# p.v of a decode attention kernel: four keys a matmul, in four column tiles of the array

## The chip, the cores and the metric

The kernel runs on one core of one Trainium2 chip. The metric is device time in microseconds (us), the median of several executions. A profiled execution gives a trace; its span is about 1.7 us shorter than the device time of the same execution (842.7 us against 844.37 us for the kernel before).

Engines are named as the profile does: PE is TensorE's matmul, PEld its weight load, DVE is VectorE, ACT is ScalarE, POOL is GpSimd, SP is SyncE (which issues the loads).

## The reference

Two independent decode steps of attention, A and B, each for one new token and 32 heads of 128. A attends to all 16384 cached keys, B to the last 4096. The outputs (512 columns each) stand side by side.

```
q = (x @ wq) split into 32 heads
scores = q . k_cache * 128**-0.5        # A: 16384 keys a head, B: 4096
p = softmax(scores)
o = p @ v_cache                         # one row of 128 per head
out = o (32*128) @ wo                   # 512 columns
```

Nearly all the bytes are K and V: with wq and wo 352 MB of bf16, each byte read once.

## The kernel before

Keys lie on partitions: 128 partitions, 128 keys on each for a head of A, 32 for a head of B. Work goes in *units* (one head of A, or four of B; 4 MB of K and 4 MB of V each) and in *chunks* of 64 keys a partition, two a unit. K and V have two 4 MB buffers each. Per chunk: DVE multiplies K by q (prod) and adds the upper to the lower half (half), PE sums on with an identity matrix (red), DVE finishes the sum (sc), ACT takes exp and its sum (p, cs), PE multiplies p by V.

```python
def _red(nc, cx, ch):                      # 8 matmuls of 512 columns a chunk
    ...
        cx.o(nc.tensor.matmul(ch.red[:, :, :], lhsT=cx.ident[:, :],
                              rhs=ch.half[:, :, b * W : (b + 1) * W], ...))

def _pv(nc, cx, ch, i):
    k0, n, st, h, first, last = ch.pieces[i]
    ...
    for c in range(n):                     # one key of each partition a matmul
        cx.o(nc.tensor.matmul(
            o_ps[0:1, 0:DH],
            lhsT=ch.p[:, k0 + c : k0 + c + 1],
            rhs=ch.unit.vt[:, ch.k0 + k0 + c, :],
            start=(first and c == 0), stop=(last and c == n - 1), ...))
        if c == 0:
            ...                            # the sum of p (fp32, 1x1)
    if ch.last_of_unit and i == len(ch.pieces) - 1:
        cx.loads.release("vt")             # the next V load may be issued
```

At a head's end: reciprocal of the sum (DVE), a scaled copy to a row (ACT), four small matmuls that turn the row into a column (PE), a cast (DVE) for each four heads, and the product with wo (PE).

The softmax here doesn't subtract the row's maximum and nothing guards it: scores larger than these inputs give would overflow.

## Time and profile before

844.42 us, median of 3 (844.36 to 844.65). What matters, and where it is read:

| reading | value | view |
|---|---|---|
| load queue q1 | 352.33 MB, 98.2% of 16 DMA engines' span | DMA queues |
| instruction queue q8 | 49 packets, 0.80 MB, 0.4% | DMA queues |
| PE, DVE, ACT busy | 68%, 70%, 8% | busy time |
| p.v matmuls | 5120 of 128 columns, 335.4 us | groups |
| granted PE clock | 0.842 | run's result |

These are lines of the page of the kernel before: busy time in us (share, count of instructions), the DMA queues (packets, MB, share of 16 engines), the chain that ended last, and groups of instructions (count | busy us, mean ns of one | idle us of the engine just before them, and what ended most of it).

```profile
PE 576.0 (68%) x6336; PEld 410.8 (49%) x6336; DVE 587.3 (70%) x344; ACT 64.7 (8%) x275; POOL 0.8 (0%) x8
...
q1 hardware_dynamic: 21188, 352.33, 98.2%
q8 instruction: 49, 0.80, 0.4%
q14 instruction: 8, 0.07, 0.0%
...
DMA 65%; DVE 20%; issue 7%; PE 6%; SPq 0%; ACT 0%; DVEq 0%
...
L146 DVE TENSOR_TENSOR prod<-kt,qallA 128x8192 bf16<-128x8192 bf16 x64 | 283.0, 4422 | 207.4 <-DMA kt<-in_A_k_cache_dram 207.3
L203 PE MATMUL o_ps<-vt,p_sb 128*1 128x128 bf16 x5120 | 335.4, 230 | 56.4 <-DMA vt<-in_A_v_cache_dram 56.4
L203 PEld LDWEIGHTS <-p_sb 128*1 128x1 bf16 x5120 | 317.4, 89 | 44.2 <-issue 44.2
L171 PE MATMUL red<-half,ident 128*128 128x512 bf16 x640 | 203.9, 476 | 16.0 <-DVE half L158 15.9
```

The kernel is bound by its loads: the load queue fills the 16 DMA engines for 98.2% of the span, and the chain is mostly DMA.

The table by windows (columns: window, length, busy of PE, PEld, DVE, ACT, POOL with counts, granted clock, DMA share, GB/s) shows the end of the kernel before:

```profile
805.00:810.00 5.00, 5.00 (x71) 4.19 (x71) 4.96 (x4) 0.35 (x2) 0.00 (x0) 0.92 1.02 424
810.00:815.00 5.00, 4.85 (x72) 3.89 (x69) 5.00 (x4) 0.35 (x2) 0.00 (x0) 1.00 0.88 369
815.00:820.00 5.00, 3.77 (x44) 2.62 (x45) 5.00 (x4) 0.36 (x1) 0.00 (x0) 1.00 0.90 359
820.00:825.00 5.00, 3.99 (x49) 2.75 (x45) 3.05 (x3) 0.53 (x4) 0.00 (x0) 1.00 1.00 419
825.00:830.00 5.00, 5.00 (x94) 5.00 (x94) 0.85 (x2) 0.89 (x5) 0.00 (x0) 1.00 0.67 272
```

At 810 to 820 us the rate dips, as a V load waits for its buffer.

### The profile page before, as it was taken

Reading aid. Unit: us, or ns where it says so; the run is one execution under the profiler, and the core shown is the slowest. Engines: PE = TensorE matmul, PEld = TensorE weight load, DVE = VectorE, ACT = ScalarE, POOL = GpSimd, SP = SyncE. Lnnn points to the kernel's source line nnn. Section 1 sums busy time; section 2 is a strip of 40 time slices with the busy share of each in tenths; the row PEclk is TensorE's granted clock in tenths of the full one; section 3 lists DMA queues with packets and bytes.
Section 4 is the critical chain, followed back from the end, with each engine's and each line's share of the span. In section 5 each row is a group of like instructions: output and inputs, shape, how many; then the busy total and the mean of one; then the engine's idle time right before and its main releaser. Section 6 shows DMA issues by size and latency. Waiting matters only on the chain.

```text
span 842.7 us, 13703 instructions
## 1 busy us (share of the span) xinstructions
PE 576.0 (68%) x6336; PEld 410.8 (49%) x6336; DVE 587.3 (70%) x344; ACT 64.7 (8%) x275; POOL 0.8 (0%) x8
## 2 busy tenths in 40 slices
PE   3377756767577665777677764677676668577687
PEld 1144544545555445445555444445454445444466
DVE  0992937779477783777867685766957779377791
ACT  2001100000000000100000000000000000000001
POOL 0000000000000000000000000000000000000000
PEclk9699787898788897888878897888898887788889
DMA  9999999999999999999999999999999999999993
GB/s 384 437 422 429 430 420 434 429 436 424 416 437 430 428 428 417 436 426 422 438 426 424 435 412 437 430 425 437 425 415 433 433 427 431 415 432 433 428 390 155
DMA packets 21533, 353.20 MB, mean 419 GB/s; under 512 B 2530, under 2 KB 2532, under 8 KB 4836
## 3 DMA queue, kind: packets, MB, share of 16 engines
q1 hardware_dynamic: 21188, 352.33, 98.2%
q8 instruction: 49, 0.80, 0.4%
q14 instruction: 8, 0.07, 0.0%
q10 hardware_dynamic: 288, 0.00, 0.0%
HBM read 352.32 MB, written 0.00 MB: 418 GB/s over the span
## 4 chain that ended last, share of the span: by engine, by line
DMA 65%; DVE 20%; issue 7%; PE 6%; SPq 0%; ACT 0%; DVEq 0%
DMA kt<-in_A_k_cache_dram 52%; DVE prod L146 13%; DMA vt<-in_A_v_cache_dram 7%; DMA kt<-in_B_k_cache_dram 6%; DVE half L158 6%; PE o_ps L203 4%; PE red L171 1%; DVE sc L183 1%; DVE recip L227 0%; PE outB L258 0%; PE oc_ps L241 0%; SPq L136 0%; PE outA L258 0%; ACT orow L229 0%; ACT rowB L269 0%
## 5 line engine op out<-in xcount | busy, mean ns | idle before, releaser
L146 DVE TENSOR_TENSOR prod<-kt,qallA 128x8192 bf16<-128x8192 bf16 x64 | 283.0, 4422 | 207.4 <-DMA kt<-in_A_k_cache_dram 207.3
L203 PE MATMUL o_ps<-vt,p_sb 128*1 128x128 bf16 x5120 | 335.4, 230 | 56.4 <-DMA vt<-in_A_v_cache_dram 56.4
L203 PEld LDWEIGHTS <-p_sb 128*1 128x1 bf16 x5120 | 317.4, 89 | 44.2 <-issue 44.2
L171 PE MATMUL red<-half,ident 128*128 128x512 bf16 x640 | 203.9, 476 | 16.0 <-DVE half L158 15.9
L158 DVE TENSOR_TENSOR half<-prod 128x4096 bf16<-128x4096 bf16 x80 | 182.5, 2281 | 0.0
L241 PE MATMUL oc_ps<-one,orow 1*32 1x1 bf16 x256 | 16.1, 171 | 173.1 <-ACT orow L229 173.1
L171 PEld LDWEIGHTS <-ident 128*128 128x128 bf16 x640 | 67.0, 115 | 110.7 <-issue 68.1
L241 PEld LDWEIGHTS <-orow 1*32 1x32 bf16 x256 | 11.5, 111 | 184.8 <-ACT orow L229 183.6
L146 DVE TENSOR_TENSOR prod<-kt,qallB 128x4096 bf16<-128x4096 bf16 x32 | 72.2, 2289 | 1.5 <-DMA kt<-in_B_k_cache_dram 0.9
L187 ACT ACTIVATE p_sb<-sc 128x64 bf16<-128x64 f32 (+1 forms) x96 | 23.5, 244 | 637.7 <-DVE sc L183 637.7
L183 DVE TENSOR_REDUCE sc<-red 128x64 f32<-128x512 f32 x80 | 54.8, 685 | 4.4 <-PE red L171 4.4
L212 PEld LDWEIGHTS o_ps<-ones_col,cs 128*1 128x1 f32 x192 | 14.7, 89 | 56.3 <-issue 56.3
L229 ACT ACTIVATE orow<-o_ps,recip 1x128 bf16<-1x128 f32 x64 | 22.1, 356 | 100.7 <-DVE recip L227 100.7
L227 DVE RECIPROCAL recip<-o_ps 1x1 f32<-1x1 f32 x64 | 9.0, 148 | 18.3 <-PE o_ps L203 18.3
L212 PE MATMUL o_ps<-ones_col,cs 128*1 128x1 f32 x192 | 19.5, 171 | 0.0
L101 PE MATMUL q_ps<-wq_t,xbA 128*128 128x512 bf16 x32 | 9.1, 455 | 13.1 <-DMA wq_t<-in_A_wq_dram 13.1
L187 ACT ACTIVATION_READ_ACCUMULATOR p_sb<-sc 128x1 f32 x96 | 17.9, 186 | 0.0
L101 PEld LDWEIGHTS <-xbA 128*128 128x128 bf16 x32 | 3.6, 114 | 18.1 <-DVE xbA L81 8.5
L101 PE MATMUL q_ps<-wq_t,xbB 128*128 128x512 bf16 x32 | 8.2, 377 | 5.3 <-ACT qallB L108 4.7
L258 PE MATMUL outB<-wo_t,oc 128*1 128x512 bf16 x32 | 8.2, 379 | 0.3 <-DVE oc L252 0.3
L258 PE MATMUL outA<-wo_t,oc 128*1 128x512 bf16 x32 | 8.2, 379 | 0.0
L101 PEld LDWEIGHTS <-xbB 128*128 128x128 bf16 x32 | 3.1, 96 | 10.1 <-issue 7.2
(17 smaller groups left out, 21.5 us busy)
## 6 DMA issues: line engine op xcount, KB each, us to landing
kt<-in_A_k_cache_dram SPq DMA_DIRECT2D x32, 4096.0 KB, 28.0
vt<-in_A_v_cache_dram SPq DMA_DIRECT2D x31, 4096.0 KB, 28.0
kt<-in_B_k_cache_dram SPq DMA_DIRECT2D x32, 1024.0 KB, 24.2
vt<-in_B_v_cache_dram SPq DMA_DIRECT2D x31, 1024.0 KB, 25.6
wq_t<-in_A_wq_dram SPq DMA_DIRECT2D x1, 4096.0 KB, 12.3
wq_t<-in_B_wq_dram SPq DMA_DIRECT2D x1, 4096.0 KB, 24.1
wo_t<-in_A_wo_dram SPq DMA_DIRECT2D x4, 1024.0 KB, 29.2
wo_t<-in_B_wo_dram SPq DMA_DIRECT2D x4, 1024.0 KB, 30.4
```

What stands on the lines that cost most here:

```text
L101: cx.o(nc.tensor.matmul(q_ps[:, :], lhsT=st.xb[:, c, :], rhs=st.wq_t[:, c, j * 512 : (j + 1) * 512], start=(c == 0), stop=(c == KC - 1),))
L146: cx.o(nc.vector.tensor_tensor(out=ch.prod[:, k0 : k0 + n, :], in0=ch.unit.kt[:, ch.k0 + k0 : ch.k0 + k0 + n, :], in1=q.rearrange("p (o d) ...
L158: cx.o(nc.vector.tensor_tensor(out=ch.half[:, :, :], in0=ch.prod[:, :, 0 : DH // 2], in1=ch.prod[:, :, DH // 2 : DH], op=ALU.add,))
L171: cx.o(nc.tensor.matmul(ch.red[:, :, :], lhsT=cx.ident[:, :], rhs=ch.half[:, :, b * W : (b + 1) * W], start=(b == 0), stop=(b == nb - 1),))
L183: cx.o(nc.vector.tensor_reduce(out=sc[:, :], in_=ch.red[:, :, :], axis=AX.X, op=ALU.add))
L187: cx.o(nc.scalar.activation(out=ch.p[:, k0 : k0 + n], in_=sc[:, k0 : k0 + n], func=ACT.Exp, scale=SCALE, accum_out=ch.cs[:, i : i + 1],))
L203: cx.o(nc.tensor.matmul(o_ps[0:1, 0:DH], lhsT=ch.p[:, k0 + c : k0 + c + 1], rhs=ch.unit.vt[:, ch.k0 + k0 + c, :], start=(first and c == 0) ...
L212: cx.o(nc.tensor.matmul(o_ps[0:1, DH : DH + 1], lhsT=ch.cs[:, i : i + 1], rhs=cx.ones_col[:, 0:1], start=False, stop=last, skip_group_chec ...
L227: cx.o(nc.vector.reciprocal(recip[:, :], o_ps[0:1, DH : DH + 1]))
L229: cx.o(nc.scalar.activation(out=orow[:, :], in_=o_ps[0:1, 0:DH], func=ACT.Copy, scale=recip[0:1, 0:1]))
L241: cx.o(nc.tensor.matmul(st.oc_ps[32 * hp : 32 * hp + 32, j : j + 1], lhsT=orow_j[:, j, :], rhs=cx.one[0:1, 0:1], start=True, stop=True,))
L258: cx.o(nc.tensor.matmul(st.out_ps[0:1, :], lhsT=st.oc[:, j : j + 1], rhs=st.wo_t[i][:, g, j * st.DN : (j + 1) * st.DN], start=(h == G - 1 ...
```

## The change

Its intent is to take load off PE: 16 matmuls of 512 columns a chunk instead of 64 of 128. A matmul takes the p of four keys as weights (4 columns) and the V of the same four keys (512 columns). Of its 4x512 result only the four diagonal blocks of 1x128 are wanted; the rest is waste that costs no extra time here. Four such matmuls go to four column tiles of the array (output partitions 0, 32, 64, 96). At a head's end the bank is copied to SBUF and four fp32 matmuls with a selecting weight column pick and sum the diagonal blocks.

```diff
 def _pv(nc, cx, ch, i):
...
-    for c in range(n):
+    T = n // 4
+    for t in range(T):
+        r = 32 * (t % 4)
+        k = k0 + 4 * t
         cx.o(nc.tensor.matmul(
-            o_ps[0:1, 0:DH],
-            lhsT=ch.p[:, k0 + c : k0 + c + 1],
-            rhs=ch.unit.vt[:, ch.k0 + k0 + c, :],
...
+            acc[r : r + 4, :],
+            lhsT=ch.p[:, k : k + 4],
+            rhs=ch.unit.vt[:, ch.k0 + k : ch.k0 + k + 4, :],
+            start=(first and t < 4),
+            stop=(last and t >= T - 4),
         ))
...
+    if last:
+        st.acc_sb[h] = cx.accs_pool.tile([P, 4 * DH], F32, tag="accs", name="acc_sb")
+        cx.o(nc.scalar.copy(st.acc_sb[h][:, :], acc[:, :]))
+
+def _fin_fold(nc, cx, st, heads):
...                                        # the sums of p, as before, then
+        for e in range(4):
+            cx.o(nc.tensor.matmul(
+                f_ps[0:1, x, 0:DH],
+                lhsT=cx.sel[:, e : e + 1],
+                rhs=acc_sb[:, e * DH : (e + 1) * DH],
+                start=False, stop=(e == 3), skip_group_check=True,
+            ))
```

The rest of the diff sets up `sel` and the two zeroed PSUM banks `acc`, and reorders the steps at a head's end so that two heads of B share them.

More of the change, by code (lines that the diff above doesn't have):

```diff
@@ L199, in _pv @@
     if first:
-        st.o_ps[h] = cx.pso_pool.tile([1, DH + 1], F32, tag="o", name="o_ps")
-    o_ps = st.o_ps[h]
-    for c in range(n):
-        cx.o(nc.tensor.matmul(
-            o_ps[0:1, 0:DH],
-            lhsT=ch.p[:, k0 + c : k0 + c + 1],
-            rhs=ch.unit.vt[:, ch.k0 + k0 + c, :],
-            start=(first and c == 0),
-            stop=(last and c == n - 1),
-            skip_group_check=True,
-        ))
-        if c == 0:
-            cx.o(nc.tensor.matmul(
-                o_ps[0:1, DH : DH + 1],
-                lhsT=ch.cs[:, i : i + 1],
-                rhs=cx.ones_col[:, 0:1],
-                start=False,
-                stop=last,
-                skip_group_check=True,
-            ))
+        cx.turn = 1 - cx.turn
@@ L220, in _pv @@
+        st.acc[h], st.cs[h] = cx.acc[cx.turn], []
+    acc = st.acc[h]
+    st.cs[h].append(ch.cs[:, i : i + 1])
+    T = n // 4
+    for t in range(T):
+        r = 32 * (t % 4)
+        k = k0 + 4 * t
+        cx.o(nc.tensor.matmul(
+            acc[r : r + 4, :],
[3 more added lines that the diff above has]
+            stop=(last and t >= T - 4),
+        ))
     if ch.last_of_unit and i == len(ch.pieces) - 1:
@@ L221, in _pv @@
         cx.loads.release("vt")
-def _fin_row(nc, cx, st, h):
-    o_ps = st.o_ps.pop(h)
-    recip = cx.small.tile([1, 1], F32, tag="recip", name="recip")
-    cx.o(nc.vector.reciprocal(recip[:, :], o_ps[0:1, DH : DH + 1]))
-    orow = cx.small.tile([1, DH], BF16, tag="orow", name="orow")
-    cx.o(nc.scalar.activation(
-        out=orow[:, :], in_=o_ps[0:1, 0:DH], func=ACT.Copy, scale=recip[0:1, 0:1]
-    ))
-    st.orow[h] = orow
+    if last:
+        st.acc_sb[h] = cx.accs_pool.tile([P, 4 * DH], F32, tag="accs", name="acc_sb")
+        cx.o(nc.scalar.copy(st.acc_sb[h][:, :], acc[:, :]))
@@ new lines, in _fin_fold @@
+def _fin_fold(nc, cx, st, heads):
+    f_ps = cx.psf_pool.tile([1, 2, DH + 1], F32, tag="f", name="f_ps")
+    for x, h in enumerate(heads):
+        cs = st.cs.pop(h)
+        for i, col in enumerate(cs):
+            cx.o(nc.tensor.matmul(
+                f_ps[0:1, x, DH : DH + 1], lhsT=col, rhs=cx.ones_col[:, 0:1],
+                start=(x == 0 and i == 0), stop=(i == len(cs) - 1), skip_group_check=True,
+            ))
+        acc_sb = st.acc_sb.pop(h)
+        for e in range(4):
+            cx.o(nc.tensor.matmul(
+                f_ps[0:1, x, 0:DH],
+                lhsT=cx.sel[:, e : e + 1],
+                rhs=acc_sb[:, e * DH : (e + 1) * DH],
+                start=False, stop=(e == 3), skip_group_check=True,
+            ))
+    return f_ps
@@ L235, in _fin_col, with _fin_row @@
+def _fin_row(nc, cx, st, heads, f_ps):
+    n = len(heads)
+    recip = cx.small.tile([1, 2], F32, tag="recip", name="recip")
+    cx.o(nc.vector.reciprocal(recip[0:1, 0:n], f_ps[0:1, 0:n, DH]))
+    for x, h in enumerate(heads):
+        orow = st.orow[h] = cx.small.tile([1, DH], BF16, tag="orow", name="orow")
+        cx.o(nc.scalar.activation(
+            out=orow[:, :], in_=f_ps[0:1, x, 0:DH], func=ACT.Copy, scale=recip[0:1, x : x + 1]
+        ))
 def _fin_col(nc, cx, st, h):
@@ L305 @@
     cx.wo_pool = pool("wo", 2)
+    cx.accs_pool = pool("accs", 2)
     cx.red_pool = pool("red", 2, **PS)
-    cx.pso_pool = pool("pso", 3, **PS)
+    cx.psf_pool = pool("psf", 1, **PS)
     cx.pst_pool = pool("pst", 1, **PS)
@@ L328 @@
     )
+    cx.sel = cx.singles.tile([P, 4], F32, tag="sel", name="sel")
+    nc.vector.tensor_reduce(
+        out=cx.sel[:, :],
+        in_=cx.ident[:, :].rearrange("p (t e) -> p e t", t=4)[:, 0:4, :],
+        axis=AX.X,
+        op=ALU.add,
+    )
+    cx.turn = 0
+    cx.acc = []
+    for i in range(2):
+        cx.acc.append(cx.psout_pool.tile([P, 4 * DH], F32, tag=f"acc{i}", name=f"acc{i}"))
+        nc.vector.memset(cx.acc[i][:, :], 0.0)
     def problem(name, x, k_cache, v_cache, wq, wo, sk0, W, at):
@@ L337, in problem @@
         st.out_ps = cx.psout_pool.tile([1, st.DN], F32, tag=f"out{name}", name=f"out{name}")
-        st.wo_t, st.o_ps, st.orow = {}, {}, {}
+        st.wo_t, st.acc, st.acc_sb, st.cs, st.orow = {}, {}, {}, {}, {}
         return st
@@ L390, in fin_pe @@
     def fin_pe():
-        for f in list(fins):
-            s, st, h = f
-            if s == 1:
-                _fin_col(nc, cx, st, h)
-                f[0] = 2 if h % G == G - 1 else 9
-            elif s == 3:
-                _fin_out(nc, cx, st, h)
+        for f in fins:
+            s, st, heads, _ = f
+            if s == 0:
+                f[3] = _fin_fold(nc, cx, st, heads)
+                f[0] = 1
+            elif s == 2:
+                for h in heads:
+                    _fin_col(nc, cx, st, h)
+                f[0] = 3 if heads[-1] % G == G - 1 else 9
+            elif s == 4:
+                _fin_out(nc, cx, st, heads[-1])
                 f[0] = 9
@@ L402, in fin_dve @@
         for f in fins:
-            s, st, h = f
-            if s == 0:
-                _fin_row(nc, cx, st, h)
-                f[0] = 1
-            elif s == 2:
-                _fin_cast(nc, cx, st, h)
-                f[0] = 3
+            s, st, heads, f_ps = f
+            if s == 1:
+                _fin_row(nc, cx, st, heads, f_ps)
+                f[0] = 2
+            elif s == 3:
+                _fin_cast(nc, cx, st, heads[-1])
+                f[0] = 4
     def pv(ch):
+        done = []
         for i, (_, _, st, h, _, last) in enumerate(ch.pieces):
@@ L414, in pv @@
             if last:
-                yield [0, st, h]
+                done.append(h)
+        if done:
+            fins.append([0, st, done, None])
     prev = None
@@ L425 @@
             waiting.append(prev)
+        fin_pe()
         _add(nc, cx, ch)
         fin_dve()
-        fin_pe()
         _red(nc, cx, ch)
         if len(waiting) > 1:
-            fins += pv(waiting.pop(0))
+            pv(waiting.pop(0))
         prev = ch
@@ L435 @@
     for ch in waiting:
-        for i, (_, _, st, h, _, last) in enumerate(ch.pieces):
-            _pv(nc, cx, ch, i)
-            fin_dve()
-            fin_pe()
-            if last:
-                fins.append([0, st, h])
+        fin_pe()
+        fin_dve()
+        pv(ch)
     while fins:
+        fin_pe()
         fin_dve()
-        fin_pe()
 _INS = ['A_x', 'A_k_cache', 'A_v_cache', 'A_wq', 'A_wo', 'B_x', 'B_k_cache', 'B_v_cache', 'B_wq', 'B_wo']
```

## The prediction

> **What bounds the kernel now.** The loads. The page's DMA queue table gives 352.33 MB on the load queue, its packets' time 98.2% of 16 engines' 842.7 us: 827.5 us. By the packet records the loads run from about 1.5 us to 833.7 us, so the DMA engines lost only about 4.7 us. Summing issued against landed bytes, 3 to 4 MB (7 to 10 us of work) are still outstanding at nearly every issue. The one starved place is the end: in the windows of 5 us the rate falls from about 425 GB/s to 369 and 359 at 810-820 us, because the last V load waits for a V buffer that the p.v of problem A's head 30 holds until 814.9. The 9 us after the last landing are compute: in the chain of waits the last B heads' p.v, 1.75 us each, row, column, cast, output matmul, store.
>
> The other engines have room: PE 68%, DVE 70%. The DVE shares in the chain (prod 13%, half 6%) lie between a landing and a buffer's release and are covered by the second buffer.
>
> **What the change removes.** 5120 p.v matmuls of 128 columns (groups: 335 us of PE; a chunk's 64 took 3.9 us warm in the timeline), replaced by 1280 of 512 columns. Streamed columns are the same. One after another they would still cost about 3.8 us a chunk (8 identity matmuls of 512 columns took 1.90 us). If the four column tiles run together, I estimate 1.0 to 1.6 us. The Trainium skill, "TensorE: Matmul & The Clock Gate", section "Measured speedup vs the span model", has 2.38x for three column tiles at 512 columns; no run here shows it yet.
>
> **What it adds.** Per head: an ACT copy of a 128x512 fp32 bank (est. 0.6 us; the 1x512 output cast took 0.57) and four fp32 matmuls of 128 columns, two PE instructions each like the present fp32 ones (192 for 96), est. 0.8 to 1.6 us a head. That is about +40 us ACT and +50 to 100 us PE, on engines with room. PE busy should fall from 576 to about 350 us (280 to 430), its granted clock from 0.84 to about 0.75.
>
> **On the critical path.** In mid-kernel nothing: V buffers come free about 2 us earlier, but the DMA queue already holds work. At the end, the last V load can be issued about 2.5 us earlier, and four heads' p.v shrink to about 0.5 us each; against that come a copy (0.8 us with hand-over) and a fold of two heads (1.7 to 3 us). From the last landing I count p.v 0.9, copy 0.8, fold 1.9, reciprocal and two rows 1.1, column and cast 0.7, output matmul and cast 1.9, store 1.9: 9.2 us, as now. Only the earlier last load gains, 1 to 2 us.
>
> **Prediction:** 842.8 us, 80% range 839.5 to 846. Faster by over 2%: 1%; within 2%: 97%; slower: 2%.
>
> **What would show it.** Right: the load queue's packet time stays about 827 us; p.v's PE time falls by half or more while the total doesn't move; DVE's wait for A's K loads stays near 207 us; the dip at 810-820 us shrinks. Wrong: packet time changes (PE's wider reading slows the loads), or a chunk's p.v takes over 6 us.
>
> **What would make it wrong.** Drains at each switch between column tiles and the 128x128 identity matmuls, slow fp32 folds ahead of the identity sums so that DVE waits, or a longer tail of single-head steps (up to +4 us).

## The result, and the profile after

839.22 us, median of 4 (838.92 to 839.76); the kernel before on the same chip 844.39 us. The ratio is 0.9939 (95% interval 0.9922 to 0.9956). Ratios here are the mean time of one kernel's runs over that of the other's of the same rounds, so not quite the ratio of the medians. The change is faster by 0.6%, within 2%, but below the lower end of the predicted range (839.5) and with three times the predicted gain.

The page of the kernel after has these lines in the places of those above:

```profile
PE 446.3 (53%) x3007; PEld 175.5 (21%) x3008; DVE 585.5 (70%) x331; ACT 98.6 (12%) x339; POOL 0.8 (0%) x8
...
q1 hardware_dynamic: 21188, 352.33, 98.7%
q8 instruction: 23, 0.38, 0.2%
q14 instruction: 9, 0.07, 0.0%
...
DMA 66%; DVE 21%; issue 9%; PE 3%; ACT 1%; SPq 0%; DVEq 0%; ACTq 0%
...
L146 DVE TENSOR_TENSOR prod<-kt,qallA 128x8192 bf16<-128x8192 bf16 x64 | 283.2, 4425 | 216.3 <-DMA kt<-in_A_k_cache_dram 216.2
L171 PE MATMUL red<-half,ident 128*128 128x512 bf16 x640 | 236.1, 535 | 286.8 <-DVE half L158 286.8
...
L209 PE MATMUL acc_101<-vt,p_sb 128*4 128x512 bf16 x640 | 58.1, 485 | 59.9 <-DMA vt<-in_A_v_cache_dram 59.9
...
L235 PE MATMUL f_ps<-acc_sb,sel 128*1 128x128 f32 x512 | 64.4, 272 | 16.2 <-ACT acc_sb L220 16.2
...
L209 PE MATMUL acc_103<-vt,p_sb 128*4 128x512 bf16 x640 | 53.1, 448 | 6.0 <-DMA vt<-in_A_v_cache_dram 6.0
```

p.v fell from 335.4 us of PE to 58.1 + 53.1 = 111.2 us. The timeline of a chunk with a warm clock (the granted clock is 1.00 there; start, length, then the group) shows the 16 matmuls in 1.03 us:

```profile
403.47 1.03 PE L209 MATMUL acc_103<-vt,p_sb 128*4 128x512 bf16 x16
```

So the column tiles do run together. PE's instruction packets (q8) fell from 49 to 23. The windows at the end:

```profile
805.00:810.00 5.00, 4.33 (x26) 1.28 (x24) 5.00 (x4) 0.63 (x2) 0.00 (x0) 0.55 1.04 439
810.00:815.00 5.00, 3.94 (x34) 1.79 (x35) 5.00 (x4) 0.56 (x3) 0.00 (x0) 1.00 1.00 423
815.00:820.00 5.00, 1.69 (x11) 0.78 (x9) 3.48 (x3) 0.54 (x4) 0.00 (x0) 0.64 0.99 411
820.00:825.00 5.00, 4.32 (x34) 1.54 (x33) 0.69 (x1) 1.01 (x5) 0.00 (x0) 0.68 0.89 365
825.00:830.00 5.00, 5.00 (x64) 2.85 (x62) 0.47 (x3) 2.61 (x7) 0.00 (x0) 1.00 0.30 120
```

The dip is gone and the loads end some 4 us earlier. From the packet records: the last load byte lands at 832.6 us of the span before and at 828.3 us after. The span fell by 842.7 - 837.5 = 5.2 us; 4.3 us of this is the earlier last landing and 0.9 us the shorter work behind it (10.1 us before, 9.2 us after). (The prediction put the last landing before at 833.7; it is 1.1 us too late.)

Why do the same bytes land 4.3 us earlier? A load's completion semaphore is raised once by each of the 16 DMA engines as its share lands (the Trainium skill, "DMA: Bandwidth & Descriptors", section "Why a DMA increments its semaphore by 16 and not by 1"; the records here do have 16 rises for each large load). The semaphore records of the trace so give, for every load, when each engine was done with its share. This is worked out from them; a line is the load whose first engine was done at about the time given (us from the first load's issue), and the 16 numbers say how much later than the first each engine was done, sorted:

```
kernel before
  at  41.0: 0.0 0.1 0.2 0.2 0.2 0.2 0.2 0.3 0.3 0.3 0.3 0.3 0.4 0.5 0.5 0.5
  at 397.7: 0.0 0.0 0.2 0.2 0.3 0.5 0.8 2.0 3.1 3.2 3.2 4.5 4.6 4.7 4.7 4.8
  at 798.1: 0.0 0.1 0.1 0.1 0.2 1.2 1.5 3.1 7.7 7.8 9.2 9.3 9.3 9.4 9.4 9.5
kernel after
  at  40.9: 0.0 0.0 0.1 0.2 0.2 0.2 0.3 0.3 0.4 0.4 0.4 0.5 0.5 0.5 0.5 0.5
  at 399.9: 0.0 0.0 0.1 0.3 0.4 0.6 1.1 1.6 1.8 1.8 2.0 2.0 2.1 2.4 3.3 3.4
  at 797.9: 0.0 0.0 0.2 0.4 0.5 1.9 2.1 3.2 3.4 3.5 4.9 5.0 5.1 5.1 5.2 5.3
```

The 16 engines start together. In the kernel before eight of them then fall behind step by step, in steps of about 1.3 to 1.6 us, by 7.7 to 9.5 us; of the other eight, five hardly do, and three by 1.2 to 3.1 us. In the kernel after the lags are smaller and run on without a gap (3.2, 3.4 us), so there the eight can't be told from those three. What holds up the three was not followed up. The leading engines are at the same place in both kernels (798.1 and 797.9 us), the last one lags 9.5 us before and 5.3 us after: 4.2 us less, which is the gain in the last landing. A load has landed only when its slowest engine is done.

The same records tie the steps to the instruction packets. Add up the 16 lags of each large load (124 loads up to 790 us, lags taken from the mean of the five leading engines) and count the q8 packets that had started by then: the sum rises by 1.62 us for each packet in the kernel before and by 1.75 us in the kernel after, with a correlation of 0.999 in both. In the runs with 42 and 84 dummy matmuls below it is 1.65 and 1.63 us. A packet's own record lasts only 1.07 us; the rest of its cost is not explained here.

### The profile page after: what moved, and what is told of

The parts are those of the page before. It is cut to its first block, busy times and chain, and to the rows that moved or that the text cites. A ratio compares the mean times of both kernels' runs of the same rounds, so it can differ in the third digit from the quotient of the medians. Undisturbed runs are those within 1.5% of the kernel's fastest.

```text
span 837.5 us, 7159 instructions
## 1 busy us (share of the span) xinstructions
PE 446.3 (53%) x3007; PEld 175.5 (21%) x3008; DVE 585.5 (70%) x331; ACT 98.6 (12%) x339; POOL 0.8 (0%) x8
## 4 chain that ended last, share of the span: by engine, by line
DMA 66%; DVE 21%; issue 9%; PE 3%; ACT 1%; SPq 0%; DVEq 0%; ACTq 0%
DMA kt<-in_A_k_cache_dram 53%; DVE prod L146 13%; DMA kt<-in_B_k_cache_dram 10%; DVE half L158 6%; DMA wq_t<-in_B_wq_dram 3%; DVE sc L183 2%; PE q_ps L101 1%; PE f_ps L235 1%; ACT qallB L108 0%; PE red L171 0%; PE acc_101 L209 0%; DVE recip L247 0%; SPq L136 0%; PE outB L278 0%; PE oc_ps L261 0%
## 5 line engine op out<-in xcount | busy, mean ns | idle before, releaser
L146 DVE TENSOR_TENSOR prod<-kt,qallA 128x8192 bf16<-128x8192 bf16 x64 | 283.2, 4425 | 216.3 <-DMA kt<-in_A_k_cache_dram 216.2
L171 PE MATMUL red<-half,ident 128*128 128x512 bf16 x640 | 236.1, 535 | 286.8 <-DVE half L158 286.8
L171 PEld LDWEIGHTS <-ident 128*128 128x128 bf16 x640 | 78.0, 123 | 404.8 <-issue 376.8
L209 PE MATMUL acc_101<-vt,p_sb 128*4 128x512 bf16 x640 | 58.1, 485 | 59.9 <-DMA vt<-in_A_v_cache_dram 59.9
L235 PE MATMUL f_ps<-acc_sb,sel 128*1 128x128 f32 x512 | 64.4, 272 | 16.2 <-ACT acc_sb L220 16.2
L209 PEld LDWEIGHTS <-p_sb 128*4 128x4 bf16 x1280 | 27.8, 91 | 147.4 <-issue 137.0
L209 PE MATMUL acc_103<-vt,p_sb 128*4 128x512 bf16 x640 | 53.1, 448 | 6.0 <-DMA vt<-in_A_v_cache_dram 6.0
L235 PEld LDWEIGHTS f_ps<-acc_sb,sel 128*1 128x1 f32 x512 | 38.2, 83 | 29.2 <-ACT acc_sb L220 18.7
L220 ACT COPY acc_sb<-acc_103 128x512 f32<-128x512 f32 x32 | 18.7, 586 | 140.0 <-PE acc_103 L209 83.1
L220 ACT COPY acc_sb<-acc_101 128x512 f32<-128x512 f32 x32 | 18.8, 588 | 127.6 <-PE acc_101 L209 86.6
L250 ACT ACTIVATE orow<-f_ps,recip 1x128 bf16<-1x128 f32 x64 | 21.2, 354 | 86.4 <-DVE recip L247 86.4
L229 PE MATMUL f_ps<-ones_col,cs 128*1 128x1 f32 x192 | 14.1, 165 | 0.0
L229 PEld LDWEIGHTS f_ps<-ones_col,cs 128*1 128x1 f32 x192 | 11.5, 85 | 11.7 <-issue 4.5
```

Source lines behind the costliest of these rows:

```text
L146: cx.o(nc.vector.tensor_tensor(out=ch.prod[:, k0 : k0 + n, :], in0=ch.unit.kt[:, ch.k0 + k0 : ch.k0 + k0 + n, :], in1=q.rearrange("p (o d) ...
L171: cx.o(nc.tensor.matmul(ch.red[:, :, :], lhsT=cx.ident[:, :], rhs=ch.half[:, :, b * W : (b + 1) * W], start=(b == 0), stop=(b == nb - 1),))
L209: cx.o(nc.tensor.matmul(acc[r : r + 4, :], lhsT=ch.p[:, k : k + 4], rhs=ch.unit.vt[:, ch.k0 + k : ch.k0 + k + 4, :], start=(first and t < ...
L220: cx.o(nc.scalar.copy(st.acc_sb[h][:, :], acc[:, :]))
L229: cx.o(nc.tensor.matmul(f_ps[0:1, x, DH : DH + 1], lhsT=col, rhs=cx.ones_col[:, 0:1], start=(x == 0 and i == 0), stop=(i == len(cs) - 1), ...
L235: cx.o(nc.tensor.matmul(f_ps[0:1, x, 0:DH], lhsT=cx.sel[:, e : e + 1], rhs=acc_sb[:, e * DH : (e + 1) * DH], start=False, stop=(e == 3), s ...
```

## The experiments

Theory A: PE's instruction packets go through eight of the 16 DMA engines, each holds its engine up, and the loads land with the engine that was held up most. The change gained by halving the PE instructions, not by making p.v faster. Theory B, the one of the prediction's small gain taken further: p.v that ends earlier frees V buffers earlier, so that loads are issued earlier and the DMA engines starve less (have no load to work on for less of the time).

In this table, "last landing" and "work behind it" are in us of the span, from the packet records; "largest lag" is that of the slowest DMA engine at about 798 us, as in the fence above (runs with larger lags hold back the leading engines too, by the buffers).

| kernel | median us (lowest to highest) | q8 packets | largest lag | last landing | work behind it |
|---|---|---|---|---|---|
| before | 844.39 (844.30 to 844.65) | 49 | 9.5 | 832.6 | 10.1 |
| after | 839.22 (838.92 to 839.76) | 23 | 5.3 | 828.3 | 9.2 |
| e1_one_tile | 845.19 (844.88 to 845.50) | 23 | 4.9 | 828.1 | 15.1 |
| e7_slow_mid | 839.11 (838.93 to 839.73) | 23 | 5.0 | 828.4 | 9.6 |
| e2_fill_pe | 843.65 (843.43 to 844.56) | 49 | 9.7 | 832.8 | 9.1 |
| e3_fill_pe2 | 852.52 (850.14 to 852.72) | 74 | 14.9 | 839.4 | 11.4 |
| e4_before_fill | 851.37 (850.97 to 852.07) | 75 | 12.5 | 839.2 | 10.1 |
| e6_bf16_fold | 837.87 (837.69 to 838.00) | 21 | 4.9 | 828.3 | 7.7 |

The runs e1 to e4 were timed beside the kernel before at 844.43 us, e6 and e7 on another chip beside it at 844.37 us, as were e5_fill_pool and e8_last_v_8eng, which are told in the text below. All gave correct results.

### One column tile

```diff
-        r = 32 * (t % 4)
+        r = 0
...
-            start=(first and t < 4),
-            stop=(last and t >= T - 4),
+            start=(first and t == 0),
+            stop=(last and t == T - 1),
```

> The kernel after with all p.v matmuls in one column tile (rows 0 to 3): the same 1280 matmuls of 512 columns and the same instruction count, but one after another, so a chunk's p.v should take about 3.8 us as before the change instead of 1.0 (warm). Theory A (the gain comes from fewer PE instructions to fetch: 23 instruction packets of 16 KB instead of 49, each of which holds up one DMA engine by over 1 us): time stays at 839.2, within 0.7 us. Theory B (the gain comes from V buffers that come free earlier): back to 842.5 or more.

The time is 845.19 us, ratio to before 1.0009 (0.9997 to 1.0022). On its face this speaks for theory B. The trace does not: p.v became as slow as foreseen,

```profile
398.00 3.62 PE L209 MATMUL acc<-vt,p_sb 128*4 128x512 bf16 x16
```

and yet the last byte landed at 828.1 us, as in the kernel after, with the same lags. All of the 6 us came after the last landing: 15.1 us of work instead of 9.2, as the last chunks' p.v, 3.62 us each, wait there for each other and for the last V. So the loads don't feel a slow p.v, while the end does. Neither theory's number for the whole time was right, since neither had counted the end.

### One column tile, but not at the end

This run tells the two parts apart: one tile for all chunks but the last six.

```diff
-        r = 32 * (t % 4)
+        r = 32 * (t % 4) if ch.tail else 0
...
-            start=(first and t < 4),
-            stop=(last and t >= T - 4),
+            start=(first and t < (4 if ch.tail else 1)),
+            stop=(last and t >= T - (4 if ch.tail else 1)),
```

> One column tile (slow p.v) everywhere but in the last 6 chunks, which use four. Theory A, with the finding that the one-tile run lost its 6 us only after the last landing: 839.2, within 0.6 us, that is the speed of p.v in mid-kernel is worth nothing. Theory B: 842 or more.

839.11 us, ratio 0.9939 (0.9927 to 0.9952): the same as the kernel after, with PE busy 71% instead of 53%. The speed of p.v in mid-kernel is worth nothing, so theory B falls as far as it rests on that speed. It leaves one part of it open: the last V load was issued at 808.3 us here and at 809.6 us in the one-tile run, about as early as in the kernel after (809.3 us), although p.v was slow. What an early issue is worth by itself is shown by the next run.

### Dummy instructions on PE

The kernel after, with 42 or 84 dummy matmuls a chunk behind p.v; each has a weight load as well. They write to an unused row of an output bank (that bank was made taller for it).

```diff
+def _fill(nc, cx, n):
+    for _ in range(n):
+        cx.o(nc.tensor.matmul(
+            cx.scratch, lhsT=cx.one[0:1, 0:1], rhs=cx.one[0:1, 0:1],
+            start=True, stop=True, skip_group_check=True,
+        ))
...
             pv(waiting.pop(0))
+            _fill(nc, cx, 42)
```

> The kernel after with 42 dummy 1x1 matmuls behind each chunk's p.v, behind the release of its V buffer: 6720 more PE instructions (each has its weight load), about as many in all as the kernel before. Theory A: about 50 instruction packets, skew between the 16 DMA engines' landings at the end about 9 us as in before, time 844.0 (843.0 to 845.5). Theory B: 839.2, within 0.7 us, as V is released as early as in the kernel after.

> As the run before with 84 dummies a chunk, 13440 more PE instructions. Theory A: about 76 instruction packets, at 0.19 us a packet above the kernel after: 849.3 (847 to 852). Theory B: 839 to 840.

With 42 the time is 843.65 us: nearly all of the gain is lost again, with 49 instruction packets as in the kernel before.

```profile
q8 instruction: 49, 0.80, 0.4%
```

The lags are those of before (largest 9.7 us) and so is the last landing (832.8 us), although p.v is fast and the release of V stands right behind it, as in the kernel after. The last V load was issued at 811.4 us, 2.1 us later than there and 3.5 us earlier than in the kernel before; the load rate does not dip (418 and 426 GB/s in the windows from 810 to 820 us, against 369 and 359 before), and still the loads land as late. So the dip was not what cost the time, and theory B falls altogether. With 84 the largest lag is 14.9 us. Theory A's sum fits it: 74 - 23 = 51 more packets over eight engines are 6.4 each, and 14.9 - 5.3 = 9.6 us of added lag is 1.5 us a packet. The time, 852.52 us, is 3 us above what was expected and just outside the expected range: the landing is 11.1 us later than in the kernel after instead of 10, and the work behind it 2.2 us longer, where 84 dummies a chunk stand in PE's way. No run followed up these excesses. For the first, the records show that in the last large loads one of the eight engines stands alone, 9.6 to 9.9 us late where the next is 8.4 to 8.6 us late. That would fit one packet more than its share.

The same dummies in the kernel before:

```diff
             fins += pv(waiting.pop(0))
+            _fill(nc, cx, 42)
```

> The kernel before with 42 dummy matmuls a chunk behind the release: about 76 instruction packets. Theory A: 5 us slower than before, 849.5 (847.5 to 852). Theory B: 844.4, within 0.7 us.

851.37 us, 6.9 us slower than before, with 75 packets. The cost belongs to the instructions, not to the new p.v. It is again somewhat above the expected value and inside the expected range.

### Dummy instructions on GpSimd

```diff
             pv(waiting.pop(0))
+            for _ in range(84):
+                cx.o(nc.gpsimd.memset(cx.junk[0:1, 0:1], 0.0))
```

> The kernel after with 84 dummy 1x1 memsets a chunk on GpSimd (6640 more GpSimd instructions, PE's untouched). If any engine's instruction fetches are as dear as PE's (they land on the same DMA engines), 844 (842.5 to 845.5); if they are spread over other DMA engines or cost no load any time, 839 to 840.5. V buffers' release is untouched, so theory B expects 839.2.

965.08 us, but the dummies themselves took the 963.3 us span (6552 of them, one each 147 ns), and the chain that ended last is GpSimd's. The loads, however, were all landed at 854.7 us, 26 us later than in the kernel after, which neither expectation had. The queues of this run:

```profile
q8 instruction: 23, 0.38, 0.2%
q14 instruction: 60, 0.49, 0.1%
```

These 51 more packets, of 8 KB, took only 0.1% of the 16 engines' time. The lags show where:

```
GpSimd dummies
  at 199.8: 0.0 0.1 0.1 0.2 0.2 0.4 0.4 0.5 0.5 0.8 1.5 1.6 1.6 1.7 1.7 7.9
  at 397.6: 0.0 0.1 0.2 0.5 0.8 0.8 1.5 1.6 1.6 1.9 2.0 2.0 2.4 3.3 3.3 15.4
  at 796.4: 0.0 0.1 0.1 0.2 0.2 0.3 0.3 0.3 0.4 0.4 0.5 0.6 0.6 1.1 2.5 16.8
```

One engine alone falls behind: GpSimd's instructions all come through it. By 400 us it is 15 us late; then the gap grows little (16.8 us at 796 us), presumably as the buffers let the others run no further ahead, and all go at its pace. This is theory A at its plainest: one DMA engine of 16 sets the landing, and a count or a share that is averaged over 16 hides it.

### The folded banks in bf16

```diff
-        st.acc_sb[h] = cx.accs_pool.tile([P, 4 * DH], F32, tag="accs", name="acc_sb")
+        st.acc_sb[h] = cx.accs_pool.tile([P, 4 * DH], BF16, tag="accs", name="acc_sb")
...                                        # and sel cast to bf16
```

> The kernel after with the banks copied out and folded in bf16: one PE instruction and one weight load for each fold matmul instead of two, 512 PE instructions fewer (about 21 instruction packets instead of 23). Theory A: 0.2 us a packet, 0.4 us from the loads, plus about 1 us from the last two heads' fold (2.0 us in the kernel after): 837.9 (837.2 to 838.6). If instruction fetches do not matter: 838.2.

837.87 us, ratio to before 0.9923 (0.9910 to 0.9937): the fastest of all, better than both kernels. The size was foreseen, the split was not quite. The last landing did not move (828.3 us): two packets fewer of 23 still leave some of the eight engines with three. All of the gain lies in the work behind it, 7.7 us instead of 9.2.

### The last V load on eight DMA engines

The last head's V was loaded as 16 loads of 8 partitions, in the hope that these go to eight engines only (the Trainium skill, "DMA: Bandwidth & Descriptors", section "Why a DMA increments its semaphore by 16 and not by 1", says that the number of engines must divide the slowest dimension and that the lowest-numbered are taken), and that these are the leading ones.

```diff
+        if cuts > 1 and st.name == "B" and which == "v":
+            for p0 in range(0, P, 8):
+                cx.o(nc.sync.dma_start(
+                    out=t[p0 : p0 + 8, i * L : (i + 1) * L, :], in_=src[p0 : p0 + 8, :, :],
+                ))
+            continue
```

> The kernel after with the very last V load (head 31 of problem B, 1 MB) issued as 16 loads of 8 partitions each. If a load of 8 partitions uses only 8 DMA engines and these are the ones that run ahead, the lagging ones have 1/8 MB less each and the last landing comes about 2 us earlier: 837.2. If they are the lagging ones: 842 or more. If it spreads over all 16: 839 to 840. Lag of the DMA engines as the cause (theory A) needs the first or the second.

848.06 us (846.46 to 848.91), ratio 1.0041; the number alone would fit "the lagging ones". But the experiment failed: the loads share eight semaphores, so most of the 16 could only be issued when earlier loads had fully landed, and their issue stretched from 808 to 831 us. The semaphore records have nine rises for each of these loads, where the other large loads have 16; that fits eight engines, as the skill says, and one more step. (That about eight packets were in flight at the end shows nothing: so it was in the kernel before.) Which eight, and whether a load can be steered away from the lagging ones, stays open.

## Why the prediction was wrong

- **The bound.** Right: the loads. Their packet time stayed, as foreseen: 827.5 us of 16 engines before, 826.8 us after. So the loads themselves did not get cheaper. DVE's wait for A's K loads went from 207.3 to 216.2 us; near 207 was foreseen.
- **PE's saving.** Right in kind: a chunk's p.v takes 1.03 us warm (predicted 1.0 to 1.6), the four tiles together 3.62 / 1.03 = 3.5 times as fast as one tile. The Trainium skill ("TensorE: Matmul & The Clock Gate", section "Measured speedup vs the span model") has 2.38 for three. PE busy in all was 446 us, outside the predicted 280 to 430. The sum was wrong by arithmetic (576 - 335 + 110 + 75 is about 425, not 350), and the identity matmuls took 236 us instead of 204 while the granted clock fell (0.842 to 0.761, predicted 0.75).
- **What it adds.** Right: the bank copy 0.59 us (predicted 0.6), the fold 1.03 us a head (predicted 0.8 to 1.6).
- **"In mid-kernel nothing."** Wrong, and this is the step that failed. That faster p.v gains nothing there is right (the run with slow p.v in mid-kernel: 839.11 us). But the change also halves PE's instructions, and their packets share the DMA engines with the loads: the largest lag grew to 5.3 instead of 9.5 us, and the last landing came 4.3 us earlier. The run with dummies brought the packets back to 49, and the landing went back to 832.8 us.
- **"The DMA engines lost only about 4.7 us."** This is an average over 16 engines (and with the records used here, loads from 2.1 to 832.6 us, it is 3.0 us). In the kernel before, half of them idled at the end while the other half was still 6 us behind. The average hid the half that mattered.
- **"Only the earlier last load gains, 1 to 2 us."** Wrong as a cause. The last V load was issued 5.6 us earlier (809.3 instead of 814.9 us), but in the run with 42 dummies it was issued 3.5 us earlier, the dip was gone too, and the landing was as late as before. The dip, read as starvation, was the leading engines running dry: in its lowest microsecond, 815 to 816, 8.7 of 16 packets of the load queue were in flight, which fits the lagging eight, which decide the landing, still at work.
- **The work behind the last landing.** The count of 9.2 us for the kernel after was right (9.2 measured). "As now" was not: the kernel before has 10.1 us, so 0.9 us were gained there. Without four tiles this work takes 15.1 us.

Of the 5.2 us that the span fell by, 4.3 us thus come from fewer instruction packets and 0.9 us from the end.

## What to carry to other kernels

A kernel that is bound by loads pays for its instructions too, since they come through the same DMA engines; look at the instruction lines of the DMA queues, and count per engine (PE's 16 KB packets over eight DMA engines, some 1.6 us of lag a packet here), not per 16. A load is done when its slowest DMA engine is done, so read the spread of the 16 completions and not only the mean share. And judge the end of a kernel, behind the last landing, by itself: there a slow p.v cost 6 us that it did not cost anywhere else.

## What the Trainium skill lacked or had wrong

- "Runtime: NRT & Kernel Launch", section "Instruction fetch mechanics", says that instructions come in blocks of 16 KiB (256 instructions) and that the cost of crossing a block is "mostly hidden". The block size agrees for PE (49 packets of 16 KB for 12672 instructions, 259 each). The cost isn't hidden in a kernel bound by loads: 26 packets more cost 843.65 - 839.22 = 4.4 us.
- The same section does not say through which DMA engines the blocks come. The runs show PE's on eight of the 16 (eight lag, by up to 9.5 us with 49 packets) and GpSimd's on one (it alone lags, by 15.4 us at 400 us). It gives 16 KiB for every engine; GpSimd's packets here were of 8 KB (51 more packets for 0.42 MB and 6552 dummies, some 128 each).
- "TensorE: Matmul & The Clock Gate", section "Measured speedup vs the span model", has no figure for four column tiles. At 512 columns with a warm clock they were 3.5 times as fast as one (1.03 against 3.62 us for 16 matmuls).
- No page read here says that the DMA engines of one core drift apart over a kernel, or that a mean DMA share hides it: 98.2% mean share stood beside a lag of 9.5 us.
